# Linear attention with a top-1 mixture of experts: turned outputs copied behind the next decays, routing's small matmuls between scores and states, VectorE's order in the passage

## The chip, the cores and the metric

The kernel runs on one core of one Trainium2 chip. The metric is the device time of one execution in microseconds (us), the median of several runs. The engines are TensorE (PE: matmuls; PEld: its weight loads), VectorE (DVE), ScalarE (ACT), GpSimd (POOL) and SyncE (SP, which issues most DMAs; a row of its queue reads SPq).

## The reference

A gated linear attention over 4 x 8 heads, 768 steps and head size 48 feeds a layer of 8 experts, of which each row takes one.

```python
for t in range(S):                                   # attention
    state = alpha[:, :, t, :, None] * state + einsum('bhd,bhe->bhde', k[:, :, t], v[:, :, t])
    y[:, :, t] = einsum('bhd,bhde->bhe', q[:, :, t], state)
x = y.transpose(0, 2, 1, 3).reshape(3072, 384)
logits = x @ w_gate + modality_bias[modality_id]     # routing
e_idx = argmax(logits, axis=1);  gate_w = softmax(logits)[e_idx]
for e in range(8):                                   # experts, F = 1024
    out[mask_e] = gate_w[mask_e, None] * (relu(x[mask_e] @ w1[e]) @ w2[e])
```

## The kernel before

**Attention.** The 3072 rows are 24 chunks of 128, six to a batch. A loop over s (lines 758 to 800) is a pipeline of steps: step s turns chunk s's decays (`turn_decay`, L226: four transposes on PE into a PSUM buffer `tr`, copied to `X` by ACT), scales the keys and queries of chunk s-1 (`scale_k`, `scale_q`), runs two scans of chunk s on VectorE (`decay`: `G` L232, `Fw` L238), turns the scaled keys of chunk s-2 (`keys`, L283, again into a `tr` buffer), makes chunk s-2's scores (`scores`, L269), and combines chunk s-3 (`combine`): `t` (L296) and its copies `UB` (L299) carry the state, `kv` (L305) is the chunk's own part of it, which VectorE adds into `S` (L308), and `y` (L318, L320) is the output, still turned. ACT copies it to `yt` (L322). In the step after, `rows` turns it back (L329) and SP writes it to DRAM as `xd`; in every second step `logits_turned` (L340) multiplies two chunks of `yt` with the gate's weights into the PSUM buffer `rt`, and `logits` (L349, L351) turns the sums back. The last chunk of a batch has no `keys` and no `kv`. There are three `tr` buffers, one `kv`, one `y` and one `rt`: who takes one waits until the instruction that read it last is done.

**Routing** runs inside these steps, by a table `later` that names the step of each piece. `route_group` adds the bias `bt` and finds each row's expert (`oh`, L409) on VectorE; `route_ranks` counts rows ahead of each row with small bf16 matmuls into `rt` (L423, L427, L431), which VectorE reads as `rk` (L432) before it makes `hi` and `OL` (L443, L444). Two experts are picked early (`route_early`, `early_places`: L505, L507, L539, L494 to L499), so that slots 0 and 1 of the expert stage can load weights (SP) and gather rows (POOL) while attention still runs. `gates` (L631) turns the softmax weights. `bias_table` makes `bt` from the modality numbers: a cast, one transpose into `kv` (L198), six VectorE instructions.

**The passage.** After the last step the last routing runs: `route_end` counts all rows (L556 to L560), finds each slot's key (L578 to L584; `diag` on VectorE, a matmul, `key` L581, `meta` L585), then the places of all rows (`OH` L590 and L596, matmuls L600, `idx` L494 on). `meta` names each slot's expert: SP reads it (L614) to issue the weights' loads (L619, L621). `idx` holds the rows that POOL gathers as `xg` (L642).

**The experts.** 19 slots of at most 256 rows: 12 in full, then the tail by its number of rows. A slot's rows are turned (`prep`, L840) and split into a high and a low part (`xH` ACT L842, `xL` VectorE L843); so are its weights, in four pieces each (`w1H`, `w2H` ACT L850; `w1L`, `w2L` VectorE L852). `layer1` runs four groups of 18 matmuls (L867, L868, L869) into `tr`, of which ACT makes `hH` (L871) and VectorE `hL` (L873); `layer2` runs 24 matmuls for each half of the rows (L888, L889, L890), ACT scales them (`os`, L893) and POOL scatters them (L820). Slot 0's first layer is different: it runs from plain weights at the end of attention (`first_layer`, L109).

**What sets the order.** PE's instructions of steps after the third keep program order (`pin`). All else is ordered when the program is built, by a scheduler with its own estimates; `issue_after(name)` lets what is inside it be placed only behind the instruction that `mark` holds under that name. Each engine then runs its instructions strictly in the order built. At the end the slots are built so:

```python
with issue_after("sc"):
    slot(0, ahead=True)
with issue_after("keys"), tc.issue_after(ms["h", 0, 3].ins):
    slot(1)
with tc.issue_after(last.ins), tc.issue_after(ms["h", 0, 1].ins):
    for i in range(2, NS0):
        slot(i)
```

`keys` is the copy L581, `key` the matmul L584, `count` the matmul L560, `last` the end of the places (L499).

Of the kernel before, what the change touches and what calls it, by code (L numbers as in the profile page):

```python
# [8 lines left out]
F32 = mybir.dt.float32  # L9
# [43 lines left out]
def attention_moe(ctx: ExitStack, tc: tile.TileContext, q, k, v, alpha, mid, wg, mb, w1, w2, out):  # L53
# [140 lines left out]
    def bias_table():  # L194
        mf = ac.tile([NU, P], F32, name="mf")
        vec.tensor_copy(mf, mi[:, :, 0])
        mp = ps.tile([P, NU], F32, name="kv")
        pe.transpose(mp, mf, ident[:NU, :NU])  # L198
        mt = ac.tile([P, NU], F32, name="mt")
        vec.tensor_copy(mt, mp)  # L200
        tmp = ac.tile([P, NU, E], F32, name="btt")
        for m in range(NM):
            sel = ac.tile([P, NU], F32, name=f"msel{m}")
            vec.tensor_scalar(sel, mt, float(m), None, op0=ALU.is_equal)
            vec.tensor_tensor(
                tmp if m else bt,
                sel.unsqueeze(2).broadcast_to([P, NU, E]),
                mbb[:, m].unsqueeze(1).broadcast_to([P, NU, E]),
                op=ALU.mult,
            )  # L210
            if m:
                vec.tensor_tensor(bt, bt, tmp, op=ALU.add)


    def seg(t, lo):
        return t.rearrange("p (a b) -> p a b", b=SEG)[:, :, lo : lo + P]
# [6 lines left out]

    def turn_decay(i):
        pa = trans(i, "a")
        (act.copy if i else vec.tensor_copy)(seg(X[i % 2][:, 1:], 0), pa)  # L226

    def decay(i):
        x, d = X[i % 2], DF[i % 2]
# [58 lines left out]
    def combine(i):  # L288
        c = i % NC
        qh, vt, sc = st[i, "q"], VT[i % NV], st[i, "s"]  # L290
        U = UB[i % 2]
        if c > 0:
            S0 = st[i, "S"]
            A = st[i, "G"][:, 1::SEG].unsqueeze(2).broadcast_to([P, NP, D])
            t1 = sb.tile([P, NP, D], F32, name="t1")
            vec.tensor_tensor(t1, S0, A, op=ALU.mult)  # L296
            for g in range(2):
                r = slice(64 * g, 64 * g + 64)
                act.copy(U[r, :, g, :D], t1[r])  # L299
        if c < NC - 1:  # L300
            kn = st[i, "n"]
            kv = ps.tile([P, NP, D], F32, name="kv")
            for h in range(H):
                r = slice(64 * (h % 2), 64 * (h % 2) + 64)
                pin(pe.matmul(kv[r, h // 2], kn[:, h // 2, r], vt[:, h, :D], start=True, stop=True))  # L305
            S1 = sb.tile([P, NP, D], F32, name="S")
            if c > 0:
                vec.tensor_tensor(S1, t1, kv, op=ALU.add)  # L308
            else:
                vec.tensor_copy(S1, kv)  # L310
            st[i + 1, "S"] = S1

        y = ps.tile([P, NP, P], F32, name="y")
        for j in range(NP):
            halves = [slice(64 * g, 64 * g + 64) for g in range(2)]
            if c > 0:
                for g, r in enumerate(halves):
                    pin(pe.matmul(y[r, j], U[:, j, g], qh[:, j], start=True, stop=False))  # L318
            for g, r in enumerate(halves):
                pin(pe.matmul(y[r, j], vt[:, 2 * j + g], sc[g][:, j], start=(c == 0), stop=True))  # L320
        yt = sb.tile([P, 2, NP, P], F32, name="yt") if i % 2 == 0 else st[i - 1, "yt"]
        act.copy(yt[:, i % 2], y)  # L322
        st[i, "yt"], st[i, "y"] = yt, yt[:, i % 2]

    def rows(i):
# [67 lines left out]
    def route_group(t0, t1):  # L393
        n = t1 - t0
        s = slice(t0, t1)
        sh = [P, n, E]

        def wide(a, m=E):
            return a[:, s].unsqueeze(2).broadcast_to([P, n, m])

        def over(a, m=E):
            return a.unsqueeze(1).broadcast_to([P, n, m])

        vec.tensor_tensor(L[:, s], L[:, s], bt[:, s], op=ALU.add)
        vec.tensor_reduce(mx[:, s], L[:, s], axis=AX.X, op=ALU.max)
        vec.tensor_tensor(ls[:, s], L[:, s], wide(mx), op=ALU.subtract)
        vec.scalar_tensor_tensor(eq[:, s], ls[:, s], 0.0, over(rev), op0=ALU.is_equal, op1=ALU.mult)
        vec.tensor_reduce(m2[:, s], eq[:, s], axis=AX.X, op=ALU.max)
        vec.tensor_tensor(oh[:, s], eq[:, s], wide(m2), op=ALU.is_equal)  # L409

    def route_ranks(t0, t1):
        n = t1 - t0
# [344 lines left out]
    for s in range(NU + 3):  # L757
# [2 lines left out]
            load(s + PF - 1)  # L760
        if s < NU:
            turn_decay(s)
        if s == NU + 1:
            first_inputs()
        if s == NU + 2:
# [9 lines left out]
            keys(s - 2)  # L775
        if s > 4 and s % 2 == 0 and s <= NU:
            logits(s - 5)
        for f, a in later.pop(s, ()):
            f(*a)
        if s > 4 and s % 2:  # L780
            logits_turned(s - 4)
        if 0 <= s - 4:
            rows(s - 4)
        if 0 <= s - 2 < NU:
            scores(s - 2)
        if s < NU:
            guard(s)
        if s == 2:
            bias_table()
            half_index()  # L790
        if s == 4:
            sp.dma_start(xd[MID : MID + 1], zr)
# [5 lines left out]
        if s == NU + 1:  # L798
            logits(s - 4)
            route_group(*GROUPS[-2])  # L800

    first_layer(1, 0, "sc", 2)
    first_layer(1, 1)
    rows(NU - 1)
# [28 lines left out]
    def prep(i):  # L833
        x = xg[i % NX]
        xH, xL = XH[i % 2], XL[i % 2]
        for name, d0, d1 in (("kv", 0, 2), ("y", 2, 3)):
            xp = ps.tile([P, d1 - d0, T], F32, name=name)
            for d in range(d0, d1):
                for u in range(2):
                    pe.transpose(xp[:, d - d0, u * P : (u + 1) * P], x[:, u, d * P : (d + 1) * P], ident)  # L840
            if i < NS0:
                act.copy(xH[:, d0:d1], xp)  # L842
                vec.tensor_tensor(xL[:, d0:d1], xp, xH[:, d0:d1].bitcast(F32), op=ALU.subtract)  # L843
            else:
                act.copy(xf[:, d0:d1], xp)
# [9 lines left out]
    def layer1(i, ahead):  # L855
# [5 lines left out]
        for j in range(4):  # L861
# [8 lines left out]
            hH = mp.tile([P, 2, T], F32R, name="hH", bufs=6)  # L870
            ms["h", i, j] = act.activation(hH, hp, AF.Relu)  # L871
            hL = mp3.tile([P, 2, T], F32R, name="hL", bufs=6)
            vec.scalar_tensor_tensor(hL, hp, 0.0, hH.bitcast(F32), op0=ALU.max, op1=ALU.subtract)  # L873
            h.append((hH, hL))
            w2s.append(split("w2", W2[:, 2 * j : 2 * j + 2]))
        ms[i] = h, w2s
# [1 line left out]
    def layer2(i, ahead):  # L878
        h, w2s = ms[i]
        g = gg[i % NX]  # L880
        for u in range(2):
            us = slice(u * P, (u + 1) * P)
            op = ps.tile([P, DM], F32, name="sc", bufs=2)
            with issue_after(("count", "key")[u] if ahead and i == 0 else None):
                for f in range(NF):
                    j, z = divmod(f, 2)
                    (hH, hL), (wH, wL) = h[j], w2s[j]
                    pe.matmul(op, hH[:, z, us], wH[:, z], start=(f == 0), stop=False)  # L888
                    pe.matmul(op, hH[:, z, us], wL[:, z], start=False, stop=False)  # L889
                    pe.matmul(op, hL[:, z, us], wH[:, z], start=False, stop=(f == NF - 1))  # L890
# [6 lines left out]
    def slot(i, ahead=False):  # L897
        layer1(i, ahead)
        if i + 1 < NS and i < NS0:
            with issue_after("count" if ahead else None):  # L900
                prep(i + 1)
        if i + 2 <= NS0:
            weights(i + 2, i % 2)
# [55 lines left out]

    with issue_after("sc"):  # L960
        slot(0, ahead=True)
    with issue_after("keys"), tc.issue_after(ms["h", 0, 3].ins):
        slot(1)
    with tc.issue_after(last.ins), tc.issue_after(ms["h", 0, 1].ins):
        for i in range(2, NS0):
            slot(i)
    flag = nc.values_load(fli[0:1, 0:1], min_val=0, max_val=2 * P)
    with tc.If(flag > 0):
# [46 lines left out]
```

## Time and profile before

| | us |
|---|---|
| median of 3 runs (443.82 to 448.17) | 446.0 |
| profiled execution, whole / its span | 445.86 / 444.0 |
| PE busy, of the span | 400.1 (90%) |
| DVE busy | 272.9 (61%) |
| ACT busy | 237.8 (54%) |
| POOL busy | 132.9 (30%) |
| mean granted PE clock | 0.947 |

Times in the views are us from the span's start. A row of a timeline is start, duration, engine, line and operation, output and inputs, shapes, count; in brackets stands how long the engine had been idle and what it waited for. A row by groups has the count, busy time and mean, and behind the second bar the idle time just before these instructions. A row by stretches has the length, the busy times of PE, PEld, DVE, ACT and POOL (with counts), the granted clock of PE (1.00 is full), the DMA engines' busy share and GB/s.

### The profile page before, as it was taken

What the parts mean: (1) busy time and instruction counts of PE and PEld (TensorE: products, weight loads), DVE (VectorE), ACT (ScalarE), POOL (GpSimd) and SP (SyncE); (2) the same over time, 40 slices, a digit from 0 to 9 for tenths busy, and PEclk for the clock granted to TensorE, in tenths of its full rate; (3) what the DMA queues carried; (4) which work ended last, traced back from release to release, by engine and by line L of the source; (5) the groups of instructions that cost most, each with busy time, mean ns of one, the idle gap of its engine ahead of it and who ended that gap; (6) DMA issues with size and microseconds to landing.
All of it is one profiled execution on the core that took longest, in us unless ns stands there. A gap on an engine that the chain in (4) does not pass through costs nothing. (4 is left out here: it accounts for less than half of the span.)

```text
span 444.0 us, 9615 instructions
## 1 busy us (share of the span) xinstructions
PE 400.1 (90%) x3659; PEld 370.0 (83%) x3659; DVE 272.9 (61%) x546; ACT 237.8 (54%) x441; POOL 132.9 (30%) x175
## 2 busy tenths in 40 slices
PE   3899998899899779998888999999999999999691
PEld 3787887788697658877777999999999999999691
DVE  7846778577868884355885665756756657542040
ACT  3447776477666544555363565655655655633130
POOL 9202222121121123500263473532533432310100
PEclk9859999699999997998998999999999999999977
DMA  8996876378747154910599866866768568301180
GB/s 154 206 184 140 179 148 150 70 171 178 157 113 162 37 207 153 335 57 0 194 385 380 301 198 196 284 225 221 208 221 280 165 203 288 115 18 37 42 290 8
DMA packets 134489, 78.37 MB, mean 177 GB/s; under 512 B 103809, under 2 KB 121278, under 8 KB 134424
## 3 DMA queue, kind: packets, MB, share of 16 engines
q1 hardware_dynamic: 130328, 67.72, 54.7%
q0 software_dynamic: 4096, 9.85, 6.0%
q8 instruction: 33, 0.54, 0.5%
q14 instruction: 32, 0.26, 0.2%
HBM read 68.10 MB, written 9.65 MB: 175 GB/s over the span
## 5 line engine op out<-in xcount | busy, mean ns | idle before, releaser
L852 DVE TENSOR_TENSOR w2L<-w2r,w2H 128x768 fp32r<-128x768 f32 x52 | 49.1, 956 | 58.1 <-ACT w2H L850 58.1
L868 PE MATMUL tr<-xL,w1H 128*128 128x256 f32 x264 | 75.4, 286 | 2.1 <-DVE xL L843 2.0
L867 PE MATMUL tr<-xH,w1H 128*128 128x256 f32 x264 | 75.4, 288 | 2.1 <-ACT xH L842 2.1
L869 PE MATMUL tr<-xH,w1L 128*128 128x256 f32 x264 | 74.8, 284 | 0.0
L274 POOL TENSOR_SCALAR_AFFINE_SELECT scT<-scT 128x512 f32<-128x512 f32 x48 | 33.8, 726 | 119.7 <-ACT scT L273 119.7
L850 ACT CAST w2H<-w2r 128x768 fp32r<-128x768 f32 x52 | 42.6, 833 | 43.4 <-PE sc L890 34.8
L820 POOL DMA_INDIRECT out_dram<-os,odx x24 | 26.7, 1113 | 127.3 <-ACT os L893 76.5
L888 PE MATMUL sc<-w2H,hH 128*128 128x384 f32 x192 | 64.5, 338 | 0.0
L890 PE MATMUL sc<-w2H,hL 128*128 128x384 f32 x192 | 62.4, 335 | 1.9 <-DVE hL L873 1.9
L889 PE MATMUL sc<-w2L,hH 128*128 128x384 f32 x192 | 64.0, 335 | 0.0
L850 ACT CAST w1H<-w1r 128x768 fp32r<-128x768 f32 x44 | 36.2, 833 | 36.5 <-PE tr L868 23.9
L852 DVE TENSOR_TENSOR w1L<-w1r,w1H 128x768 fp32r<-128x768 f32 x44 | 41.7, 958 | 22.3 <-ACT w1H L850 22.3
L868 PEld LDWEIGHTS tr<-xL,w1H 128*128 128x128 f32 x264 | 50.9, 193 | 2.6 <-DVE xL L843 2.6
L867 PEld LDWEIGHTS tr<-xH,w1H 128*128 128x128 f32 x264 | 50.9, 194 | 2.3 <-ACT xH L842 2.3
L869 PEld LDWEIGHTS tr<-xH,w1L 128*128 128x128 f32 x264 | 51.0, 193 | 0.0
L873 DVE SCALAR_TENSOR_TENSOR hL<-tr,hH 128x512 fp32r<-128x512 f32 x46 | 31.3, 684 | 13.3 <-ACT hH L871 13.3
L642 POOL DMA_INDIRECT xg<-xd,idx x26 | 30.0, 1154 | 26.9 <-DVE vals L495 9.3
L320 PE MATMUL y<-scT,vt 128*64 128x128 f32 x384 | 38.0, 285 | 0.0
L890 PEld LDWEIGHTS sc<-w2H,hL 128*128 128x128 f32 x192 | 35.9, 188 | 2.3 <-DVE hL L873 2.3
L888 PEld LDWEIGHTS sc<-w2H,hH 128*128 128x128 f32 x192 | 36.2, 189 | 0.5 <-issue 0.5
L889 PEld LDWEIGHTS sc<-w2L,hH 128*128 128x128 f32 x192 | 36.2, 189 | 0.1
L647 POOL DMA_INDIRECT gg<-gd,idx x26 | 30.6, 1179 | 13.4 <-issue 6.7
(224 smaller groups left out, 770.0 us busy)
## 6 DMA issues: line engine op xcount, KB each, us to landing
w1r<-in_moe_w_dram SPq DMA_DIRECT2D x28, 768.0 KB, 6.2
w2r<-in_moe_w_dram SPq DMA_DIRECT2D x28, 768.0 KB, 8.1
nat_a<-in_alpha_dram SPq DMA_DIRECT2D x24, 192.0 KB, 3.2
nat_k<-in_k_dram SPq DMA_DIRECT2D x24, 192.0 KB, 3.4
nat_q<-in_q_dram SPq DMA_DIRECT2D x24, 192.0 KB, 3.5
vt<-in_v_dram SPq DMA_DIRECT2D x24, 192.0 KB, 3.0
xd<-xs SPq DMA_DIRECT2D x24, 192.0 KB, 2.8
xg<-xd,idx POOLq DMA_INDIRECT x26, 5.8
```

What stands on the lines that cost most here:

```text
L274: pool.affine_select(s, s, [[0, NP], [1, P]], ALU.is_ge, 0.0, base=0, channel_multiplier=-1)
L320: pin(pe.matmul(y[r, j], vt[:, 2 * j + g], sc[g][:, j], start=(c == 0), stop=True))
L647: pool.indirect_dma_start(gg[i % NX][:, u : u + 1], None, gd[0:rows], ix, bounds_check=rows - 1, oob_is_err=False)
L850: act.copy(hi, src)
L852: vec.tensor_tensor(lw, src, hi.bitcast(F32), op=ALU.subtract)
L867: pe.matmul(hp[:, z], wH[:, d, fs], xH[:, d], start=(d == 0), stop=False)
L868: pe.matmul(hp[:, z], wH[:, d, fs], xL[:, d], start=False, stop=False)
L869: pe.matmul(hp[:, z], wL[:, d, fs], xH[:, d], start=False, stop=(d == ND - 1))
L873: vec.scalar_tensor_tensor(hL, hp, 0.0, hH.bitcast(F32), op0=ALU.max, op1=ALU.subtract)
L888: pe.matmul(op, hH[:, z, us], wH[:, z], start=(f == 0), stop=False)
L889: pe.matmul(op, hH[:, z, us], wL[:, z], start=False, stop=False)
L890: pe.matmul(op, hL[:, z, us], wH[:, z], start=False, stop=(f == NF - 1))
```

## The change

No arithmetic is added or left out. Six edits move work:

1. The copy of `yt` leaves `combine` for a function of its own, `outputs`, called a step later behind `turn_decay` and held behind the copy of `X`.
2. The pieces in `later` (ranks, counts, tables, gates) are called behind `scores` instead of ahead of `logits_turned`.
3. `bias_table` is made in steps 5 and 6 instead of step 2, with its transpose pinned in program order.
4. In the passage, slot 0's `hL` of groups 1 to 3 are held behind the last `oh`.
5. Slot 0's second layer is held behind `count` for its first three steps f of the first half, and behind `key` from there on. `prep(1)` is held behind `keys`.
6. Slots 1 to 11 are held behind `last`, `xH` and `key`, where slot 1 was held behind `keys` and a copy `hH` of slot 0.

```diff
     def bias_table():
         vec.tensor_copy(mf, mi[:, :, 0])
+        yield
-        pe.transpose(mp, mf, ident[:NU, :NU])
+        pin(pe.transpose(mp, mf, ident[:NU, :NU]))
...
     def turn_decay(i):
         pa = trans(i, "a")
-        (act.copy if i else vec.tensor_copy)(seg(X[i % 2][:, 1:], 0), pa)
+        turned = (act.copy if i else vec.tensor_copy)(seg(X[i % 2][:, 1:], 0), pa)
+        if i:
+            mark["X"] = turned
...
+        st[i, "yp"] = y
+
+    def outputs(i):
         yt = sb.tile([P, 2, NP, P], F32, name="yt") if i % 2 == 0 else st[i - 1, "yt"]
-        act.copy(yt[:, i % 2], y)
+        with issue_after("X"):
+            act.copy(yt[:, i % 2], st[i, "yp"])
...
+        mark["oh"] = vec.tensor_tensor(oh[:, s], eq[:, s], wide(m2), op=ALU.is_equal)
...
         if s < NU:
             turn_decay(s)
+        if 0 <= s - 4:
+            outputs(s - 4)
...
-        for f, a in later.pop(s, ()):
-            f(*a)
         if s > 4 and s % 2:
             logits_turned(s - 4)
         if 0 <= s - 4:
             rows(s - 4)
         if 0 <= s - 2 < NU:
             scores(s - 2)
+        for f, a in later.pop(s, ()):
+            f(*a)
...
-        if s == 2:
-            bias_table()
+        if s == 5:
+            table = bias_table()
+            next(table)
+        if s == 6:
+            next(table, None)
             half_index()
...
+    outputs(NU - 1)
     first_layer(1, 0, "sc", 2)
...
-                act.copy(xH[:, d0:d1], xp)
+                mark["xH"] = act.copy(xH[:, d0:d1], xp)
...
-            vec.scalar_tensor_tensor(hL, hp, 0.0, hH.bitcast(F32), op0=ALU.max, op1=ALU.subtract)
+            with issue_after("oh" if plain and j else None):
+                vec.scalar_tensor_tensor(hL, hp, 0.0, hH.bitcast(F32), op0=ALU.max, op1=ALU.subtract)
...
-            with issue_after(("count", "key")[u] if ahead and i == 0 else None):
-                for f in range(NF):
-                    j, z = divmod(f, 2)
-                    (hH, hL), (wH, wL) = h[j], w2s[j]
+            for f in range(NF):
+                j, z = divmod(f, 2)
+                (hH, hL), (wH, wL) = h[j], w2s[j]
+                with issue_after(("key" if u or f > 2 else "count") if ahead and i == 0 else None):
...
-            with issue_after("count" if ahead else None):
+            with issue_after("count" if ahead else None), issue_after("keys" if ahead else None):
                 prep(i + 1)
...
-    with issue_after("keys"), tc.issue_after(ms["h", 0, 3].ins):
-        slot(1)
-    with tc.issue_after(last.ins), tc.issue_after(ms["h", 0, 1].ins):
-        for i in range(2, NS0):
+    with tc.issue_after(last.ins), issue_after("xH"), issue_after("key"):
+        for i in range(1, NS0):
             slot(i)
```

The built order shows three places. The changed kernel's rows carry its own line numbers, some 1 to 14 higher. First, ACT around one step's turned decays (`scT` are the masked scores' copies, `junk` a range check of the decays, `lts` the turned logits, `xs` the rows), before and now:

```order
L299 COPY UB_158<-t_1694 64x4x48 x2
L322 COPY yt<-y 128x512
L226 COPY X_148<-tr 128x4x128
L285 COPY knat<-tr 128x512
L331 COPY xs<-tr 128x384
L242 ACTIVATE junk,gacc<-nat_a_76,bhi 128x384
```

```order
L302 COPY UB_158<-t_1694 64x4x48 x2
L227 COPY X_148<-tr 128x4x128
L329 COPY yt<-y 128x512
L288 COPY knat<-tr 128x512
L338 COPY xs<-tr 128x384
L245 ACTIVATE junk,gacc<-nat_a_76,bhi 128x384
```

The two copies have changed places; the state's copies `UB` stay ahead of both. Second, PE in a step with ranks, from the turned keys to the next `kv`, before and now:

```order
L283 MATMUL tr<-ident,kh 128x128 x4
L423 LDWEIGHTS tri
L423 MATMUL rt<-oh,tri 128x48
...
L431 MATMUL rt<-ohs,ones 128x48
L340 MATMUL rt<-yt,wgp 32x256 x4
L329 MATMUL tr<-ident,yt 128x128 x4
L269 MATMUL sc<-qh,kh 128x128 x8
L305 MATMUL kv<-vt_104,knat 64x48 x8
```

```order
L286 MATMUL tr<-ident,kh 128x128 x4
L347 MATMUL rt<-yt,wgp 32x256 x4
L336 MATMUL tr<-ident,yt 128x128 x4
L272 MATMUL sc<-qh,kh 128x128 x8
L430 LDWEIGHTS tri
L430 MATMUL rt<-oh,tri 128x48
...
L438 MATMUL rt<-ohs,ones 128x48
L308 MATMUL kv<-vt_104,knat 64x48 x8
```

The ranks have moved behind turned logits, rows and scores. Third, VectorE in the passage from the keys on (tiles with 112 and 113 belong to slots 0 and 2, with 114 and 115 to slots 1 and 3), before and now:

```order
L581 CAST key<-rt 128x34
L852 TENSOR_TENSOR w1L<-w1r_114,w1H 128x768 x3
L590 TENSOR_TENSOR OH<-key,hi 128x8x34 x3
L585 CAST meta<-rt 1x17
L852 TENSOR_TENSOR w1L<-w1r_114,w1H 128x768
L852 TENSOR_TENSOR w2L<-w2r_115,w2H 128x768 x2
...
L596 TENSOR_TENSOR OH<-OH,tok_187 128x8x34 x2
L873 SCALAR_TENSOR_TENSOR hL<-tr,hH 128x512
L494 TENSOR_SCALAR idx<-rt 128x34
```

```order
L597 TENSOR_TENSOR OH<-key,hi 128x8x34 x3
L592 CAST meta<-rt 1x17
L603 TENSOR_TENSOR OH<-OH,tok_187 128x8x34 x3
L501 TENSOR_SCALAR idx<-rt 128x34
...
L865 TENSOR_TENSOR w1L<-w1r_114,w1H 128x768 x4
L635 TENSOR_SCALAR sm<-sm 128x6
L865 TENSOR_TENSOR w2L<-w2r_115,w2H 128x768 x4
L865 TENSOR_TENSOR w1L<-w1r_112,w1H 128x768 x2
...
L865 TENSOR_TENSOR w2L<-w2r_113,w2H 128x768
L887 SCALAR_TENSOR_TENSOR hL<-tr,hH 128x512
```

The places now stand ahead of all splits of slot 1, and slot 1's first `hL`, which stood ahead of the places, stands behind all splits of slot 1 and five of slot 2.

More of the change, by code (lines that the diff above doesn't have):

```diff
@@ L408, in route_group @@
         vec.tensor_reduce(m2[:, s], eq[:, s], axis=AX.X, op=ALU.max)
-        vec.tensor_tensor(oh[:, s], eq[:, s], wide(m2), op=ALU.is_equal)
+        mark["oh"] = vec.tensor_tensor(oh[:, s], eq[:, s], wide(m2), op=ALU.is_equal)
     def route_ranks(t0, t1):
```

## The prediction

> **What bounds the kernel now.** I read the busy time by stage first, then TensorE's waits by line, then single steps in the timelines.
>
> ```profile
> 32.00:200.00 168.00, 153.84 (x1982) 130.51 (x1980) 118.01 (x295) 103.25 (x225) 38.62 (x52) 0.96 0.61 151
> 200.00:246.00 46.00, 38.03 (x256) 35.73 (x257) 30.45 (x74) 21.91 (x35) 13.79 (x11) 0.93 0.69 246
> 246.00:410.00 164.00, 164.00 (x1182) 164.00 (x1182) 97.72 (x126) 93.82 (x146) 63.38 (x55) 1.00 0.60 196
> ```
>
> Behind the length of a stretch stand the busy times of PE, PEld, DVE, ACT and POOL, then the granted clock. From 246 on PE is busy all the time at full clock: nothing in this change helps there. So time can be won only in the attention steps, where PE idles 14.2 us, and in the passage, where it idles 8.0. The groups by line say for whom it waits in the steps:
>
> ```profile
> L283 PE MATMUL tr<-ident,kh 128*128 128x128 f32 x72 | 11.5, 283 | 6.1 <-ACT X L226 6.1
> L340 PE MATMUL rt<-yt,wgp 128*32 128x256 f32 x96 | 8.3, 419 | 4.9 <-DVE rk L432 3.8 <-DVE vals L495 0.4 <-ACT gs L633 0.3
> L423 PE MATMUL rt<-oh,tri 128*128 128x48 bf16 (+2 forms) x5 | 0.9, 180 | 0.9 <-DVE vals L495 0.9
> L631 PE MATMUL rt<-ident,gt 128*18 128x128 f32 x1 | 0.4, 385 | 0.4 <-DVE rk L432 0.4
> L505 PE MATMUL rt<-ohs,ones 128*128 128x8 bf16 x2 | 0.3, 166 | 1.1 <-DVE L L351 1.1
> ```
>
> The last number of a row is idle time of PE. These five rows are 13.4 of the 14.2 us, and the change moves every one of them. A second price stands in the clock:
>
> ```profile
> 18.00:31.70 13.70, 13.70 (x75) 11.41 (x74) 6.51 (x14) 5.45 (x12) 1.73 (x3) 0.50 0.97 192
> 72.70:79.50 6.80, 4.89 (x79) 4.21 (x78) 5.43 (x17) 4.09 (x10) 1.22 (x2) 1.00 0.65 139
> 79.50:86.30 6.80, 6.80 (x68) 5.78 (x62) 3.29 (x8) 2.69 (x7) 1.22 (x2) 0.50 0.16 44
> 158.00:164.80 6.80, 4.83 (x80) 4.25 (x75) 5.57 (x28) 3.64 (x8) 1.61 (x3) 1.00 0.69 237
> 164.80:171.60 6.80, 6.45 (x57) 4.79 (x59) 2.82 (x13) 2.19 (x6) 1.86 (x2) 0.50 0.94 342
> 239.90:243.30 3.40, 3.23 (x13) 2.94 (x14) 1.46 (x3) 0.27 (x2) 2.44 (x2) 0.50 1.05 378
> ```
>
> Each half-clock stretch follows one in which PE waited often (4.89 and 4.83 busy of 6.80 us). Then PE is busy throughout, so 6.8 us at half rate lose about 3.4 us of work.
>
> **Outputs behind the next decays.** One step shows this edit and the next.
>
> ```profile
> 117.65 0.71 ACT L299 COPY UB<-t 64x192 f32<-64x192 f32 x2 [1.11 <-DVE t L296]
> 118.39 0.59 ACT L322 COPY yt<-y 128x512 f32<-128x512 f32 x1
> 118.87 0.59 ACT L226 COPY X<-tr 128x512 f32<-128x512 f32 x1
> 119.51 0.66 PE L283 MATMUL tr<-ident,kh 128*128 128x128 f32 x4 [0.59 <-ACT X L226]
> 120.16 0.18 PE L431 MATMUL rt<-ohs,ones 128*128 128x48 bf16 x1
> 121.47 0.64 PE L340 MATMUL rt<-yt,wgp 128*32 128x256 f32 x8 [1.13 <-DVE rk L432]
> 121.23 0.20 DVE L432 TENSOR_TENSOR rk<-rt,oh 128x48 f32<-128x48 f32 x1
> 121.86 1.23 DVE L238 TENSOR_TENSOR_SCAN Fw<-X,DF 128x516 f32<-128x516 f32 x1
> 123.06 0.95 DVE L444 TENSOR_TENSOR OL<-ioh,lo 128x768 f16<-128x768 f16 x1
> 124.83 0.55 DVE L296 TENSOR_TENSOR t<-S,G 128x192 f32<-128x192 f32 x1
> ```
>
> L283 needs the tr buffer that X reads, and X starts 0.48 us after yt (118.87 less 118.39). With X ahead, L283 can start 0.48 earlier. The 6.1 us are ten waits, eight of at least 0.48 and two of 0.22 and 0.23: 8 x 0.48 + 0.45 = 4.3 us come back. The rest (1.8) stays: there ACT's UB copies, late for t, are the last to end. The price: yt ends 0.48 later. In a step with L283 that time passes under L283; in the three steps without it that still turn decays (the last chunk of a batch has no keys) L340 or the turned rows stand right behind the turned queries and wait 0.48: 1.4. Sum -2.9; bounds -6.1 (all waits go) and +1.4 (none does). No instruction is added.
>
> **Routing's matmuls behind the scores.** Before, L340 writes the one rt buffer and waits until rk has read the ranks (1.13 us here, 3.8 in three steps). Now L340, the turned rows and the scores come first, and behind the ranks stand kv and y, which use other buffers. All 3.8 go. What is late next is VectorE: rk and OL (0.95) now fall between its last scan and t, and ACT's UB copies and X wait for t. By the durations above, t would start near 124.2 in this step and X end near 126.1, where the turned queries end near 125.8: 0.3 us in each of three following steps. Sum -2.9; bounds -3.8 and, if all of OL's 0.95 is waited for in each, -0.9.
>
> In the later steps (tables, gates, counts) the waits of L340 for vals and gs, of L423, L631 and L505 are 0.7 + 0.9 + 0.4 + 1.1 = 3.1. Against them the places (L494) now stand behind the scan Fw, so I put 0.75 on L423 and 0.3 on L631, and 0.4 on the matmul of the flag (L663), which comes right behind the counts and waits for their two reads: -1.7; bounds -3.1 (no new wait) and +0.6 (three of a whole scan, 1.23). The counts and places come some 2 us later so, and with them SP's loads and POOL's gathers for slots 0 and 1, which wait for their results. Their first readers (L116, L109, the casts of slot 1) stand a step or more behind in the rows: nothing.
>
> **The bias table.**
>
> ```profile
> 17.52 0.24 PE L198 MATMUL kv<-ident,mf 24*128 24x24 f32 x1 [1.38 <-DVE mf L196]
> 47.53 0.67 PE L305 MATMUL kv<-vt,knat 128*64 128x48 f32 x16
> 47.86 1.23 DVE L238 TENSOR_TENSOR_SCAN Fw<-X,DF 128x516 f32<-128x516 f32 x1
> ```
>
> The wait of 1.38 goes. In step 6 the transpose sits ahead of L305 and takes the only kv buffer; VectorE empties it (L200) behind Fw, which ends at 49.1. So L305 slips from 47.5 to about 49.2, less its own matmul 1.5 us. Sum +0.1; bounds -1.4 (the slip is made good by VectorE) and +1.5 (the old wait was covered by the half clock there).
>
> **The clock.** Without 1.9 us of waits before 79.5 I count that stretch as gone (-3.4); of the one at 164.8, where by the sums above some 1.2 of 2.0 us of waits stay, half (-1.7). Sum -5.1; bounds 0 and -6.8. [...]
>
> **The passage.**
>
> ```profile
> 213.82 0.15 DVE L585 CAST meta<-rt 1x17 int32<-1x17 f32 x1
> 214.82 1.06 SPq L619 DMA_DIRECT2D w1r<-in_moe_w_dram  x2
> 220.12 1.57 ACT L850 CAST w1H<-w1r 128x768 fp32r<-128x768 f32 x2 [4.64 <-DMA w1r<-in_moe_w_dram]
> 223.56 0.69 DVE L873 SCALAR_TENSOR_TENSOR hL<-tr,hH 128x512 fp32r<-128x512 f32 x1 [3.26 <-ACT hH L871]
> 224.17 0.18 DVE L494 TENSOR_SCALAR idx<-rt 128x34 int32<-128x34 f32 x1
> 225.25 2.69 DVE L852 TENSOR_TENSOR w1L<-w1r,w1H 128x768 fp32r<-128x768 f32 x3
> 224.94 0.28 PE L867 MATMUL tr<-xH,w1H 128*128 128x256 f32 x1
> 231.27 0.44 PE L890 MATMUL sc<-w2H,hL 128*128 128x384 f32 x1 [1.93 <-DVE hL L873]
> 237.06 0.27 PE L840 MATMUL kv<-ident,xg 128*128 128x128 f32 x1
> 239.96 1.01 PE L867 MATMUL tr<-xH,w1H 128*128 128x256 f32 x3 [2.08 <-ACT xH L842]
> ```
>
> Ahead of the count two hL move behind oh on VectorE: L423 comes sooner, but rk now has them in front, and the count waits for rk as before: nothing.
>
> The key matmuls move from behind one half of slot 0's second layer into its first nine matmuls, and VectorE does keys, xL, tables and places before any split of slot 1. meta comes near 209.5, SP issues slot 2's weights near 210.4 (4.4 earlier), and idx comes near 214, ten us earlier; so slot 2's rows are gathered in time, though POOL's gathers now run beside the weights' loads, and the wait of 2.08 goes. But VectorE then does four w1L and four w2L of slot 1 and five splits of slot 2 before slot 1's first hL: 13 x 0.9 (2.69 for three) from 215.1 on, hL ends near 227.5 instead of 224.25. The fourth group of slot 1's first layer needs its tr buffer and starts there instead of 224.94; PE does three groups from about 216.2 (18 matmuls at 164.00 / 1182 = 0.14 us, 7.5 in all) and slot 2's transposes, and then idles some 3 us, a new wait. From 224.94 to 237.06 it had 12.1 us less the 1.93 wait, 10.2 of work: slot 2 starts near 237.7, with 1.7 for a half-clock stretch behind the new wait 239.4. Before, it started at 239.96 and lost 1.7 to the half clock: 241.6. Sum -2.2; bounds -5 (no new wait) and +2, if slot 2's weights land no earlier and hold the splits, and so hL, 4.4 longer.
>
> **The sum** against the profiled execution's 445.86 us (1.9 around its span, 0.1 under the median of 446.0): -2.9 - 2.9 - 1.7 + 0.1 - 5.1 - 2.2 = -14.7, 431.2 us; I say 431.
>
> **The rivals.**
> First: the waits go, but the clock falls as often as before, at other places (a stretch begins also where PE waits only 1.4 us, ahead of 18.0). Then the clock's 5.1 is missing: 436.3. For it: two new waits of 1.5 and 3 us. [...]
>
> Second: with the 1.38 us wait gone, the clock doesn't fall at 18.0, where 13.7 us run at half rate. That is at most 6.8 more; as loads take 0.97 of the DMA engines there, I count 5: 426. Against it: the start is thin in other places too.
>
> Third, on the other side: yt behind X is late for PE in all 24 steps. Where ACT is on time there is little room:
>
> ```profile
> 105.15 0.58 ACT L322 COPY yt<-y 128x512 f32<-128x512 f32 x1
> 105.72 0.59 ACT L226 COPY X<-tr 128x512 f32<-128x512 f32 x1
> 106.95 0.64 PE L340 MATMUL rt<-yt,wgp 128*32 128x256 f32 x8
> ```
>
> X can start no earlier than 105.72, as its transposes end then; yt would end near 106.8, and L340 starts at 106.95: 0.1 to spare. If every step waits 0.59, that is 14.2 against 4.3 for X and 6.7 for the other terms, the clock staying as it is: 449. It decides from 11.0 / 24 = 0.46 us a step.
>
> That the order isn't what the diff says can't be: the built rows show it.
>
> **How the numbers follow.** Forecast 0.60, first rival 0.19, second 0.12, third 0.07, something else 0.02. The sum's open ends (some 3 us of VectorE's lateness in routing steps, 3 in the passage, 3 of clock) make 426 to 438 its own range. Reaching to the first two rivals it is 424 to 441. About 1% is what a measurement of this kernel can tell from no change (441.5 and 450.5): faster 0.85 (0.58, 0.15 and 0.12 of the first three cases), same 0.09 (what is left of these two and of the rest), slower 0.06 (nearly all of the third).
>
> **What would show it.** Right: no wait of L340 for rk; L283's waits under 2.5 us in all; full clock at the first two rank steps; a wait near 1.5 us before kv of step 6; idx within 15 us of the last count; PE waiting about 3 us for slot 1's first hL, none for slot 2's xH. Wrong: waits of L340 or the turned rows for yt in most steps, new half-clock stretches before 200 us, or slot 2's matmuls no earlier against the last count than now.

## The result, and the profile after

The changed kernel takes 431.32 us (median of 4 runs, 426.76 to 432.30); before, 445.81 us (median of 4, 443.82 to 448.17). The ratio is 0.965, 95% interval 0.957 to 0.974: faster by 2.6 to 4.3%. Forecast were 431.0 us and a range of 424 to 441. The profiled execution took 430.76 us. In the lists below, the ratios leave out runs more than 1.5% above the fastest of their kernel, so a ratio and the quotient of two medians can differ.

The total came out as forecast, but its parts did not. By cores, span and mean granted clock, before and after:

```profile
core 0: 444.0 us, clock 0.947
```

```profile
core 0: 428.9 us, clock 0.974
```

What the clock took is the span times what is missing from 1: 444.0 x 0.053 = 23.5 us before, 428.9 x 0.026 = 11.2 now. So up to 12.3 of the 15.1 us between these two executions are clock, where the prediction had 5.1. The execution profiled before was a poor draw, though: over the 53 runs of the kernel before whose clock is on record, the mean clock is 0.959 and the same product 18.1 us; over ten runs of the changed kernel they are 0.975 and 10.7. On average that is 7.4 of 13.3 us, and rather an upper bound: among the 53 runs a microsecond more of it goes with only 0.6 us more time. PE's timeline shows for the two profiled executions where the time went. The rows are the scores of chunk 2, the count, and slot 2's first matmul; before (its third, at 239.96, stands in the prediction) and after:

```profile
32.79 0.94 PE L269 MATMUL sc<-qh,kh 48*128 48x128 f32 x12
...
201.76 0.17 PE L556 MATMUL rt<-ohs,ones 128*128 128x8 bf16 x1 [0.27 <-DVE rk L432]
```

```profile
26.51 0.71 PE L272 MATMUL sc<-qh,kh 48*128 48x128 f32 x8
...
187.77 0.17 PE L563 MATMUL rt<-ohs,ones 128*128 128x8 bf16 x1 [1.04 <-DVE rk L439]
...
225.27 0.28 PE L880 MATMUL tr<-xH,w1H 128*128 128x256 f32 x1
```

| stretch | before, us | after, us | difference | half-clock time before / after |
|---|---|---|---|---|
| start to chunk 2's scores | 32.79 | 26.51 | -6.3 | 13.65 / 3.4 |
| to the count | 168.97 | 161.26 | -7.7 | 13.65 / 0 |
| to slot 2's first matmul | 38.20 | 37.50 | -0.7 | 3.4 / 6.8 |
| to the end | 204.04 | 203.63 | -0.4 | 16.3 / 12.3 |

Half of the half-clock time is counted as what a busy PE loses, an estimate from the granted 0.50 (before, slot 2's first-layer matmuls start 0.21 us apart in the stretch at 239.92 and 0.12 apart behind it): 5.1 of the 6.3 us at the start and 6.8 of the 7.7 in the steps. What is left for the waits in the steps is 0.9 us. Counted directly, PE idles 15.7 us in the steps before (168.97 less 153.29 busy) and 13.4 after (161.26 less 147.89), 2.3 less; so the waits' part is 0.9 to 2.3. The start's other 1.2 us are hardly waits (PE's idle time there goes from 8.2 to 8.0): the record of the clock begins with its first full-clock stretch, at 14.64 us before and at 10.38 after, and ahead of it PE is slower too: the transposes of a group mostly start 213 ns apart there, as in the half-clock stretches, and 109 ns apart at full clock. The same four transposes, before and after:

```profile
12.41 1.06 PE L221 MATMUL tr<-ident,nat_q 128*128 128x128 f32 x4
```

```profile
12.06 0.66 PE L222 MATMUL tr<-ident,nat_q 128*128 128x128 f32 x4
```

The windows of the changed kernel follow. Behind the length stand the busy times of PE, PEld, DVE, ACT and POOL, the clock, DMA share and GB/s. The first row is the stage of the steps, the others are the half-clock window left at the start, and two full-clock windows, each with the half-clock window that follows it:

```profile
32.00:200.00 168.00, 154.57 (x1974) 131.08 (x1973) 126.13 (x331) 105.81 (x227) 37.70 (x51) 0.99 0.62 154
...
17.20:20.60 3.40, 3.40 (x18) 2.41 (x16) 1.68 (x3) 2.05 (x6) 1.23 (x2) 0.50 1.09 219
184.46:187.87 3.41, 1.46 (x13) 0.91 (x12) 3.13 (x12) 0.49 (x2) 0.00 (x0) 1.00 0.00 0
187.87:191.28 3.41, 3.41 (x14) 2.75 (x13) 2.04 (x14) 0.47 (x1) 0.00 (x0) 0.50 0.00 0
211.77:215.18 3.41, 1.33 (x11) 1.36 (x12) 3.41 (x6) 0.80 (x1) 2.80 (x3) 1.00 1.04 378
215.18:218.59 3.41, 3.41 (x15) 3.41 (x15) 3.31 (x6) 1.37 (x3) 0.26 (x1) 0.50 1.05 384
```

PE idles 13.4 us between 32 and 200 now, 14.2 before, but 200 us lies behind the count now; over the same work it is the 13.4 against 15.7 from above. The waits have shrunk little, most have moved. The groups by line (L286 was L283, L347 was L340, L430 was L423, L308 was L305, L563 was L556) show where to:

```profile
L308 PE MATMUL kv<-vt,knat 128*64 128x48 f32 x320 | 14.1, 228 | 1.5 <-DVE mt L201 1.5
L286 PE MATMUL tr<-ident,kh 128*128 128x128 f32 x80 | 12.9, 283 | 4.7 <-ACT X L227 4.7
L347 PE MATMUL rt<-yt,wgp 128*32 128x256 f32 x96 | 7.7, 391 | 2.6 <-ACT yt L329 2.6
...
L430 PE MATMUL rt<-oh,tri 128*128 128x48 bf16 (+2 forms) x6 | 1.1, 188 | 2.6 <-DVE oh L416 2.2 <-DVE vals L502 0.4
...
L563 PE MATMUL rt<-ohs,ones 128*128 128x8 bf16 x1 | 0.2, 166 | 1.0 <-DVE rk L439 1.0
```

The 3.8 us for rk are gone. X still costs 4.7 where 2.7 were forecast (1.8, and 0.9 behind the ranks), yt 2.6 where 1.4 were. The kv wait of 1.5 is as forecast. The waits for oh and for the count's rk (2.2 and 1.0) are mostly not new. Before, they stood just behind 200 us:

```profile
201.26 0.18 PE L423 MATMUL rt<-oh,tri 128*128 128x16 bf16 x1 [2.05 <-DVE oh L409]
```

The passage, in the rows of VectorE, SP's queue and PE:

```profile
195.59 0.16 DVE L592 CAST meta<-rt 1x17 int32<-1x17 f32 x1
...
196.58 1.05 SPq L626 DMA_DIRECT2D w1r<-in_moe_w_dram  x2
...
200.50 0.19 DVE L501 TENSOR_SCALAR idx<-rt 128x34 int32<-128x34 f32 x1 [3.71 <-PE rt L607]
...
213.02 0.68 DVE L887 SCALAR_TENSOR_TENSOR hL<-tr,hH 128x512 fp32r<-128x512 f32 x1
...
213.84 0.36 PE L880 MATMUL tr<-xH,w1H 128*128 128x256 f32 x1 [2.99 <-DVE hL L887]
```

Against the count, meta comes 4.2 us earlier than before (7.8 instead of 12.1), idx 9.7 earlier (12.7 instead of 22.4), and hL 3.5 later (25.3 instead of 21.8). PE waits 2.99 us for hL, the half clock follows, and the wait for slot 2's xH is gone: the passage went as the prediction said. One of its signs of being wrong was a new half-clock stretch before 200 us. The stretch at 187.87 lies before 200, but it stands right behind the count, as the one at 202.38 did before, and isn't new.

### The profile page after: what moved, and what is told of

Read it like the earlier page. It is cut to its first block, busy times and chain, and to the rows that moved or that the text cites. A ratio compares the mean times of both kernels' runs of the same rounds, so it can differ in the third digit from the quotient of the medians.

```text
span 428.9 us, 9635 instructions
## 1 busy us (share of the span) xinstructions
PE 387.4 (90%) x3659; PEld 358.1 (83%) x3659; DVE 275.6 (64%) x546; ACT 237.1 (55%) x441; POOL 133.3 (31%) x175
## 5 line engine op out<-in xcount | busy, mean ns | idle before, releaser
L277 POOL TENSOR_SCALAR_AFFINE_SELECT scT<-scT 128x512 f32<-128x512 f32 x48 | 32.8, 703 | 114.5 <-ACT scT L276 114.4
L833 POOL DMA_INDIRECT out_dram<-os,odx x24 | 27.3, 1137 | 126.1 <-ACT os L907 90.3
L323 PE MATMUL y<-scT,vt 128*64 128x128 f32 x384 | 36.1, 274 | 0.0
L884 ACT ACTIVATE hH<-tr 128x512 fp32r<-128x512 f32 x46 | 27.2, 593 | 14.5 <-PE tr L882 8.7
```

Source lines behind the costliest of these rows:

```text
L277: pool.affine_select(s, s, [[0, NP], [1, P]], ALU.is_ge, 0.0, base=0, channel_multiplier=-1)
```

## The experiments

**One edit at a time.** Four kernels, each the kernel before with a part of the change. In this series the kernel before took 444.71 us (24 runs). First, edit 1 alone:

```diff
-        act.copy(yt[:, i % 2], y)
+        st[i, "yp"] = y
+
+    def outputs(i):
+        with issue_after("X"):
+            act.copy(yt[:, i % 2], st[i, "yp"])
```

> The kernel before with the first edit alone: the outputs' copy behind the next X. The prediction's step: 2.9 us faster, so about 443, with the wait of the turned keys for X falling from 6.1 to 1.8 us and new waits of the turned logits for yt of 1.4. The rival, read from the trace of the whole change (4.7 us for X, 2.6 for yt): what X wins, yt takes back, 445 to 448, no difference.

448.69 us (444.20 to 455.88, 6 runs), ratio 1.016 (1.008 to 1.023): not faster, and somewhat slower. Yet the waits did nearly what the edit was costed at. PE's groups in the steps:

```profile
L285 PE MATMUL tr<-ident,kh 128*128 128x128 f32 x72 | 11.5, 282 | 2.3 <-ACT X L226 2.3
L346 PE MATMUL rt<-yt,wgp 128*32 128x256 f32 x96 | 7.7, 390 | 6.8 <-DVE amin L238 3.1 <-ACT yt L328 1.8 <-DVE ohs L446 1.2
```

X fell from 6.1 to 2.3 us and yt costs 1.8 (1.8 and 1.4 were forecast). The 3.1 and 1.2 that the row puts on amin and ohs are the old rk waits: in its timeline rk ends at 76.27 and L346 starts at 76.41; ohs and amin are only the next instructions on VectorE, and neither reads rt. The count came 2.8 us earlier. Then all was lost behind it: PE waited 8.15 us for slot 2's xH, where before 2.08.

Second, edit 2 alone:

```diff
-        for f, a in later.pop(s, ()):
-            f(*a)
         if s > 4 and s % 2:
             logits_turned(s - 4)
...
             scores(s - 2)
+        for f, a in later.pop(s, ()):
+            f(*a)
```

> The kernel before with the second edit alone: routing's pieces behind the scores. The prediction's step: the waits for rk go (2.9 us net), 1.7 of the later waits, and 5.1 of half clock behind them: 436. Rival: the waits go but the clock falls as often elsewhere: 441. A look at the granted clock around the first and the last rank step tells which.

442.96 us (435.43 to 445.82, 12 runs), ratio 0.996 (0.991 to 1.002): the same. The groups:

```profile
L283 PE MATMUL tr<-ident,kh 128*128 128x128 f32 x72 | 11.6, 284 | 9.4 <-ACT X L226 9.4
L340 PE MATMUL rt<-yt,wgp 128*32 128x256 f32 x96 | 7.7, 391 | 1.6 <-ACT yt L322 1.6
```

The two rows waited 6.1 + 4.9 = 11.0 us before, and wait 9.4 + 1.6 = 11.0 here: every microsecond for rk came back as one for X. One step of its timeline shows how:

```profile
120.22 0.18 DVE L432 TENSOR_TENSOR rk<-rt,oh 128x48 f32<-128x48 f32 x1
...
121.75 0.95 DVE L444 TENSOR_TENSOR OL<-ioh,lo 128x768 f16<-128x768 f16 x1
...
122.62 0.34 DVE L296 TENSOR_TENSOR t<-S,G 128x192 f32<-128x192 f32 x1
...
123.00 0.71 ACT L299 COPY UB<-t 64x192 f32<-64x192 f32 x2 [1.99 <-DVE t L296]
...
123.74 0.59 ACT L322 COPY yt<-y 128x512 f32<-128x512 f32 x1
124.22 0.59 ACT L226 COPY X<-tr 128x512 f32<-128x512 f32 x1
...
124.86 0.66 PE L283 MATMUL tr<-ident,kh 128*128 128x128 f32 x4 [0.91 <-ACT X L226]
```

VectorE's rank rows, rk to OL, now stand between its last scan and t; t holds UB, UB holds yt and X, and X holds PE. But the attention's two half-clock stretches (79.5 and 164.8) did not occur in this profile, and the count came 5.5 us earlier. Behind it PE waited 5.91 us for slot 2's xH.

Third, edit 3 alone:

```diff
-        if s == 2:
-            bias_table()
+        if s == 5:
+            table = bias_table()
+            next(table)
+        if s == 6:
+            next(table, None)
             half_index()
```

> The kernel before with the third edit alone: the bias table in steps 5 and 6. The prediction's step: 0.1 us, so 446, a wait of 1.4 us in step 2 gone and one of 1.5 us in step 6 new. The rival, its second rival and what the trace of the whole change suggests: the half-clock stretch at the start shrinks from 13.7 to about 3.4 us, worth 5 us: 441.

446.75 us (444.48 to 453.96, 6 runs), ratio 1.012 (1.006 to 1.018): the same within 2%. Its start shows no half clock in the record (before, 13.65 us of it), though 3.41 us follow at 42.33, behind the new kv wait of 1.46; its count comes 4.8 us earlier, and then PE waits 9.07 us in the passage:

```profile
236.77 1.01 PE L871 MATMUL tr<-xH,w1H 128*128 128x256 f32 x3 [9.07 <-ACT xH L846]
```

Fourth, edits 4 to 6 alone, the passage (the last of them shown; no run separates the three):

```diff
-    with issue_after("keys"), tc.issue_after(ms["h", 0, 3].ins):
-        slot(1)
-    with tc.issue_after(last.ins), tc.issue_after(ms["h", 0, 1].ins):
-        for i in range(2, NS0):
+    with tc.issue_after(last.ins), issue_after("xH"), issue_after("key"):
+        for i in range(1, NS0):
```

> The kernel before with the edits to the passage alone. The prediction's step: 2.2 us faster, 443.6, with a new wait of PE of 3 us for slot 1's first hL and a half-clock stretch behind it, and none for slot 2's xH. Rival: the new wait and its half clock take back all of it, 446.

440.36 us (436.93 to 445.37, 12 runs), ratio 0.998 (0.992 to 1.003): the same within 2%. In its profile the hL wait is 2.77 us and the xH wait is gone; the start and the steps have as much half clock as before. Its count comes 2.5 us later all the same; why was not pursued.

So the edits don't add up. With edit 1, 2 or 3 alone the count came 2.8 to 5.5 us earlier, and without edits 4 to 6 the passage, which the scheduler orders afresh for each program, gave it back. How much of the advance is the edits' own these single profiles don't show: ahead of the count they have 20.5, 13.7 and 10.2 us of half clock where the kernel before had 27.3, and half of that difference (3.4 to 8.5 us) covers all of it.

**One edit taken out of the whole.** This asks what each edit is worth beside the others. The changed kernel itself, run a second time (below), gave ratios of 0.965 and 0.973, so that total times this close say little, and the waits have to decide. First, the whole change without edits 4 to 6:

```diff
-    with tc.issue_after(last.ins), issue_after("xH"), issue_after("key"):
-        for i in range(1, NS0):
+    with issue_after("keys"), tc.issue_after(ms["h", 0, 3].ins):
+        slot(1)
+    with tc.issue_after(last.ins), tc.issue_after(ms["h", 0, 1].ins):
+        for i in range(2, NS0):
```

> The whole change without its edits 4 to 6 (the passage is built by the rules of before). By the prediction's sum the passage is worth 2.2 us by itself, so about 433.5 us, some 2 above the changed kernel, with PE's wait for slot 2's xH near the 2.1 us of before. Theory two: the passage is worth more once the steps before it have changed, since the build then puts the second slot's xH late, as in the kernels with one of edits 1 to 3 alone (waits of 5.9 to 9.1 us): that wait is 6 to 9 us with a half-clock stretch behind it, and the time 437 to 441 us.

437.83 us (433.95 to 439.62, 4 runs), ratio 0.985 (0.975 to 0.994). Theory two holds in the wait and the median. ACT and PE in the passage:

```profile
227.30 1.56 ACT L863 CAST w2H<-w2r 128x768 fp32r<-128x768 f32 x2 [3.06 <-DMA w2r<-in_moe_w_dram]
...
228.77 0.58 ACT L855 CAST xH<-kv 128x512 fp32r<-128x512 f32 x1
...
229.40 1.01 PE L880 MATMUL tr<-xH,w1H 128*128 128x256 f32 x3 [8.31 <-ACT xH L855]
```

PE had turned slot 2's rows by 221, but xH stands on ACT behind a pair of weight casts that themselves wait for their load. In the changed kernel the same xH runs at 210.64, ahead of the next cast that waits for a load (2.75 us, at 214.38). By the medians the passage's edits are worth 6.5 us here (437.83 less 431.32), not the 2.2 that were counted. Why the loads land so late in this order was not tried.

Second, the whole without edit 1 (`act.copy(yt[:, i % 2], y)` back in `combine`):

> The whole change without edit 1 (yt is copied inside combine again, ahead of X). By the prediction 2.9 us slower than the changed kernel, about 434 us, with L283's waits for X near 6 us. Theory two, from the trace of the changed kernel, where X and yt together are waited for 7.3 us against 6.4 before: edit 1 is worth nothing beside the others, 430 to 432 us. Both: no wait for rk, no change in the passage.

432.40 us (429.78 to 436.72, 4 runs), ratio 0.977 (0.968 to 0.985). The total cannot tell this from the changed kernel; the waits can:

```profile
L284 PE MATMUL tr<-ident,kh 128*128 128x128 f32 x68 | 11.0, 285 | 8.0 <-ACT X L227 7.9
L341 PE MATMUL rt<-yt,wgp 128*32 128x256 f32 x96 | 7.7, 391 | 1.5 <-ACT yt L323 1.5
```

9.5 us against 4.7 + 2.6 = 7.3: edit 1 is worth 2.2 in waits (-2.9 was counted), and the count comes 2.8 later without it. Theory two, that it is worth nothing, falls for the waits. In the total it stays open: this profile had no half clock before 216 us, the changed kernel's had 6.8.

Third, the whole without edit 3 (the table in step 2 again):

> The whole change without edit 3 (the bias table in step 2 again). By the prediction's sum 0.1 us faster than the changed kernel, 431. By its second rival the wait of 1.4 us in step 2 is what the start's half clock hangs on: then some 13 us of half clock come back near 18 us, the kv wait of 1.5 us in step 6 is gone, and the time is about 5 us longer, 436.

431.26 us (427.96 to 431.66, 4 runs), ratio 0.968 (0.961 to 0.976). PE at the start, and windows by stretch:

```profile
17.27 0.29 PE L198 MATMUL kv<-ident,mf 24*128 24x24 f32 x1 [2.46 <-DVE mf L196]
```

```profile
13.78:17.19 3.41, 1.03 (x7) 0.67 (x6) 3.38 (x7) 1.33 (x3) 0.64 (x1) 1.00 0.89 176
17.20:30.85 13.65, 13.58 (x72) 11.25 (x73) 6.46 (x15) 4.93 (x12) 1.90 (x3) 0.50 1.03 203
211.76:215.17 3.41, 1.73 (x11) 1.40 (x11) 3.41 (x6) 2.99 (x7) 2.80 (x3) 1.00 1.05 385
```

The half clock of 13.65 us is back at the start, as the prediction's second rival had it, and the count comes 4.0 us later. Over all 14 profiles: with the table in step 2 the start has 10.2 to 13.7 us of half clock on record in 5 of 5, with the table moved none in 5, 3.4 in 2 and 10.2 in 1 of 9; in the ninth (`i_hold0`, below) the half rate ahead of the record lasts to 22.07 us (four transposes still take 1.12 us at 20.89, 0.66 at 23.56). Moving the table has a price that no term had: in 3 of the 7 profiles with it in steps 5 and 6 a half-clock stretch of 3.41 us follows the new kv wait, at 42 us. Without edit 3 the time did not grow. In its profile that is because it escaped both later stretches (neither the wait behind the count nor its hL wait of 2.25 us brought the clock down; PE was busy 2.00 us in the window of the one, 1.73 and 2.39 in the two of the other) and has no kv wait.

Fourth, the whole without edit 2 (the pieces of `later` ahead of `logits_turned` again):

> The whole change without edit 2 (ranks, counts, tables and gates ahead of the turned logits again), the only one of its edits not yet undone in the whole. By the prediction 2.9 and 1.7 us of waits come back, and with them one or two half-clock stretches in the attention steps: 435 to 440 us, with L346 waiting 3.8 us for rk. Theory two, from the kernels with one edit alone: moving the ranks trades waits for rk against waits for X, since VectorE's rank rows then stand ahead of t; X and L346 together wait about 9.1 us without edit 2 (7.3 with it), so only 1.8 us come back: 432 to 434 us, and near it if no half-clock stretch comes back.

435.20 us (429.87 to 437.75, 6 runs), ratio 0.979 (0.971 to 0.986):

```profile
L286 PE MATMUL tr<-ident,kh 128*128 128x128 f32 x68 | 10.8, 282 | 1.4 <-ACT X L227 1.3
L347 PE MATMUL rt<-yt,wgp 128*32 128x256 f32 x96 | 8.1, 410 | 6.0 <-DVE amin L239 4.3 <-ACT yt L329 0.9 <-DVE vals L502 0.4
```

The two rows wait 7.4 us, with edit 2 they wait 7.3. Its count came 3.8 us later, of which a half-clock stretch of 6.8 us at 154.7 is 3.4. So both theories had a half right: the median is the prediction's (435 to 440), though its range overlaps the changed kernel's, and the waits are theory two's. What difference there is lies in the clock: over its six runs the mean is 0.966, over ten of the changed kernel 0.975.

**The clock.** The changed kernel once more, with no edit:

> The changed kernel once more, unchanged. Theory: the granted clock is set on a fixed grid of 3.41 us that is not tied to the program's start; a window in which PE is busy under about 1.5 us is followed by one or more at half clock, one over 2.4 us is not, and between these it may go either way. Then the waits are those of the first profile (X 4.7 us, yt 2.6, oh 2.2, hL 3.0, each within 0.3, where no half clock covers them), but with the grid elsewhere the half-clock stretches of 187.9 and 215.2 us may be missing or come at other waits, and the time lies anywhere from 426 to 433 us. Rival: the clock follows the order of work alone; then the stretches come at the same places, within 0.5 us.

430.71 us (427.50 to 439.24, 6 runs), ratio 0.973 (0.964 to 0.981); its profiled execution took 427.50. In the profiles the clock changes at steps of 3.41 us, a grid (see the last section). In the ten profiles taken before this run, between 10 and 395 us, all 19 full-clock windows of the grid in which PE was busy 1.5 us or less were followed by half clock, and none in which it was busy 2.4 us or more. Here the grid lay 0.2 us earlier (17.02 where it was 17.21), and most waits were the first profile's to 0.2 us; others moved (yt at 164 us 0.48 where it was 1.20, X at 109 us 0.29 for 0.64, hL 2.50 for 2.99). The first two stretches came again, the third did not:

```profile
208.16:211.57 3.41, 1.73 (x11) 1.41 (x11) 3.41 (x6) 2.97 (x7) 2.80 (x3) 1.00 1.05 386
211.57:214.98 3.41, 2.17 (x18) 2.20 (x19) 3.41 (x6) 0.84 (x1) 2.53 (x2) 1.00 1.04 376
```

```profile
212.81 0.35 PE L880 MATMUL tr<-xH,w1H 128*128 128x256 f32 x1 [2.50 <-DVE hL L887]
```

The wait of 2.50 us, from 210.31 to 212.81, fell over two windows, 1.26 and 1.24 us in each; in the first profile 2.07 of 2.99 fell into one (211.77 to 213.84). So whether a wait of 2 to 3 us costs a stretch seems to depend on where the grid cuts it; these are two executions.

**Two mends.** First, the table two steps later, where chunk 5 has no `kv` of its own:

```diff
-        if s == 5:
+        if s == 7:
             table = bias_table()
             next(table)
-        if s == 6:
+        if s == 8:
             next(table, None)
```

> The whole change with the table's cast in step 7 and its transpose in step 8, which has no kv of its own (chunk 5 is the last of its batch) and no sum into S. If the kv buffer is what the wait of 1.5 us in step 6 hangs on, that wait is gone and the steps behind come about 1.4 us earlier: 430 us, and no half clock at the start beyond the changed kernel's. If the wait only moves to step 8 (y behind the transpose, or the state behind VectorE's six instructions), no change: 431.

425.77 us (425.43 to 431.00, 4 runs), ratio 0.962 (0.953 to 0.971). The kv wait is gone and nothing waits in its place:

```profile
46.85 0.67 PE L308 MATMUL kv<-vt,knat 128*64 128x48 f32 x16
...
52.88 0.24 PE L199 MATMUL kv<-ident,mf 24*128 24x24 f32 x1
...
59.12 0.67 PE L308 MATMUL kv<-vt,knat 128*64 128x48 f32 x16
```

Its profile has one half-clock stretch before the tail where the changed kernel has three; that, and not the 1.5 us alone, is how this execution lies 5 lower. In the total the mend is not shown: its ratio's interval overlaps the changed kernel's (0.957 to 0.974). Second, slots 2 and up behind slot 1's first hH:

```diff
-        for i in range(1, NS0):
-            slot(i)
+        slot(1)
+        with tc.issue_after(ms["h", 1, 0].ins):
+            for i in range(2, NS0):
+                slot(i)
```

> The whole change, and slots 2 and up also held behind the first hH of slot 1, so that slot 1's first hL stands ahead of the five splits of slot 2 on VectorE. If hL is late only because of these five splits (5 x 0.9 = 4.5 us), PE's wait of 3.0 us for it falls under 0.5, the half clock behind it is gone too, and the time is 3.0 to 4.7 us less than the changed kernel's: 427. Rival: the splits of slot 2 then come late in turn and PE waits for w1L or xL of slot 2 instead, no gain: 431.

427.47 us (425.24 to 431.08, 6 runs), ratio 0.964 (0.957 to 0.971). The wait of 3 us is gone, and the longest left between 196 and 240 us is 0.56, in the second layer:

```profile
210.13 0.68 DVE L887 SCALAR_TENSOR_TENSOR hL<-tr,hH 128x512 fp32r<-128x512 f32 x1
```

Against its count (189.38) hL comes 20.8 us later where it was 25.3. These 4.5 us are the five splits of slot 2 at 0.9 each, which now stand behind it: they were what made hL late. Both mends together:

> The whole change with the bias table in steps 7 and 8 and with slots 2 and up held behind the first hH of slot 1. The two should add: no kv wait (1.5 us), no hL wait (3.0 us): 422 to 425 us. If they don't add, because the new order of the passage or the clock takes it back, 426 as with the table alone.

423.88 us (422.02 to 427.13, 6 runs), ratio 0.956 (0.949 to 0.963), the lowest median of all; all its runs lie below the 427.50 that was the lowest of the unchanged repeat in the same series. hL and PE's one wait from 205 to 228 us:

```profile
208.29 0.68 DVE L887 SCALAR_TENSOR_TENSOR hL<-tr,hH 128x512 fp32r<-128x512 f32 x1
```

```profile
214.90 0.44 PE L904 MATMUL sc<-w2H,hL 128*128 128x384 f32 x1 [0.74 <-DVE w1L L865]
```

This even with 10.2 us of half clock at its start in the profiled execution.

## Why the prediction was right in its total and wrong in its parts

- **Outputs behind the next decays (-2.9).** Right in mechanism and nearly in size: -2.2 in waits beside the other edits, X down to 2.3 us with edit 1 alone. Of the 4.7 us that X still costs in the whole, 3.3 are edit 2's: without it X costs 1.4.
- **Routing behind the scores (-2.9).** The step that failed. "X end near 126.1, where the turned queries end near 125.8: 0.3 us in each of three following steps" is too little: in the step shown X made PE wait 0.91, and over the steps edit 2 adds 3.3 us of waits for X where 0.9 were counted, alone (6.1 to 9.4) as beside the others (1.4 to 4.7). There yt adds 1.7 (0.9 to 2.6), which was in no term of this step. The rk wait came back as waits for X and yt; apart from vals and gs (0.7) the two rows wait 6.7 us without edit 2 and 7.3 with it. The bound of -0.9 was nearer than the value taken, and still too good.
- **The later routing (-1.7).** Without edit 2 L430, L638, L512 and L563 wait 4.9 us and L347 0.7 for vals and gs; with it these and the flag's matmul wait 4.6: -1.0.
- **The bias table (+0.1).** The kv wait was 1.46 for the 1.5 counted. What it buys was put into the second rival, at 12 in 100: the half clock at the start. It is mostly gone, 10.2 us less here, some 5 us of time. The price of the kv wait's own half-clock stretch (3 of 7 profiles) was in no term. This rival should have had more of the chance: the 13.7 us stood right behind the wait that the edit removes.
- **The clock (-5.1).** In the steps it was -6.8 between the two profiles: both stretches went. Together with the start, 11.9 of the 15.1 us are clock there; over the runs it is 7.4 of 13.3 at most, so a part of the 11.9 is the draw of the profile before. The prediction's list left out the stretch at 202.38, behind the count, which stayed. The waits ahead of the stretches were short: no wait of PE between 10 and 400 us in the profile before was longer than 2.08 us, and five stretches at half clock began there (18.05, 79.49, 164.83, 202.38 and 239.92).
- **The passage (-2.2).** Sized right for the step from before to after: slot 2's first matmul comes 0.7 us earlier against the count, and 1.7 us of half clock behind it are gone, -2.4. Of this the tail gave 1.5 back (27.5 us for 26.0), which was in no term; its wait is 4.84 for 4.17, and the other 0.8 stays open. The new hL wait is 2.99 for 3, meta 4.2 earlier for 4.4, idx 9.7 for 10. What was not seen is that "before" is no fixed ground: with one of edits 1 to 3 alone the passage has 5.9 to 9.1 us of waiting for xH, with all three 8.3.

So waits worth 7.4 us were counted at the start and in the steps (2.9 + 2.9 + 1.7 - 0.1) where 2.1 to 2.5 came (6.3 - 5.1 and 7.7 - 6.8; by PE's idle time, 0.2 and 2.3), and clock worth 5.1 where 11.9 came. The two errors nearly cancel: that the total came so close is luck. The third rival (yt late in all steps) is excluded by yt's 2.6 us; the first (the clock falls as often elsewhere) by the mean clock of 0.975 over ten runs, 0.959 before.

## What to carry to other kernels

When short waits of PE are taken away, cost the clock first: list the windows in which PE idles most, and ask for each edit which of them it fills. A wait removed from one engine's queue is only worth what the next engine in the chain has to spare: here rk's rows went from PE's path into VectorE's, and came back as waits for X and yt. And where a scheduler orders a later stage afresh, an edit in an early stage is judged only together with the rules that hold the later stage.

## What the runs showed of the hardware

In the 14 profiles of this case the granted clock changed on a fixed grid: every half-clock stretch, but for the last, which the end cuts, was one, two, three or four times 3.41 us long, and the starts in a profile differed by multiples of 3.413 (17.21, 187.87, 215.18, 406.33 in the changed kernel). The grid's place against the program moved between executions (the first stretch began at 17.02 in `a_again`, 17.21 in the changed kernel's first profile, 17.47 in `i_both`, 18.05 in the kernel before). Over these profiles, between 10 and 395 us, of 23 full-clock windows in which PE was busy under 1.6 us 22 were followed by half clock; from 1.6 to 2.4 us 14 of 68; from 2.4 us on none of some 1400. What decides between 1.6 and 2.4 is open, and so is what ends a stretch: in the kernel before PE was busy throughout all four windows of the first (13.65 us). The record begins with the first full-clock stretch (at 10.2 to 15.0 us in 13 profiles, at 22.07 in `i_hold0`); ahead of it single transposes mostly take 417 to 421 ns where they take 272 to 273 at full clock, and the mean clock counts that time as full.

This goes some way to explain the spread of runs: the kernel before took 437.41 to 450.97 us over 24 runs, and by the granted 0.50 a busy PE loses an estimated 1.7 us in one window of 3.41 us. Over its 53 runs the time and what the clock took go together (correlation 0.76). A single profile's half-clock stretches are one draw, so a term of the clock is better counted as the number of thin windows times the share of them that fall than as a list of places.
